# Products with v in quarters of the array for two pairs at once, in two accumulators, in an fp32 attention and feed-forward kernel

## The chip, the cores and the metric

One core of one Trainium2 chip runs the whole kernel. The metric is the device time of one execution in microseconds, the median of several runs. A profile of one further execution stands beside it.

## The reference

```python
def _attn_ref(q, k, v):                       # 8 x 12 heads, 448 keys, 64 wide
    scores = scale * np.matmul(q, k.transpose(0, 1, 3, 2)) - np.log(S)
    attn = 1.0 / (1.0 + np.exp(-scores))
    return np.matmul(attn, v).astype(np.float32)

def _moe_ref(x, w_in, w_out):                 # 3584 x 768, 768 x 2048, 2048 x 768
    h = x @ w_in
    g = np.maximum(0.01 * h, h)
    return (g @ w_out).astype(np.float32)

# attention's output, heads side by side, is x of the second
```

The attention has sigmoids in place of a softmax, so that no sum over the keys has to be divided by.

## The kernel before

The kernel has three stages. Attention is the first: 48 pairs of heads, two pairs in a round, 24 rounds. The two other stages are the two products of the feed-forward part, computed by schemes with fewer block products than the plain one; their weights need sums of blocks, and these are made by VectorE (DVE) during attention (the generator `prep`, tiles `wr`, `wd`, `ws`, `w`). So do the sums of attention's results (`x`, `x_s`), which the second stage multiplies.

In a pair, one head lies on partitions 0 to 63 and the other on 64 to 127 (`heads`). Q and k (`qk`, raw) are split by ScalarE (ACT, a cast, `high`) and DVE (a subtraction, `low`) into a high and a low part (`qks`). The 448 keys are three tiles of 128 and a last one of 64. The work of a pair on TensorE (PE) has three kinds:

- `scores`: for a key tile, high x high, high x low and low x high for both heads, six matmuls of 64 rows and 128 columns of the array (64*128 in a profile), into a PSUM tile `sc` of two banks. ACT makes the sigmoid into `s`.
- `attn_v`: v with `s` in plain fp32, three key tiles for two heads. A matmul has 128 rows and 64 columns (128*64): the two heads use the two halves of the array's columns. Both pairs of a round accumulate in one PSUM tile `pv`, a bank each.
- `last_scores` and `last_v`: the last 64 keys of both pairs together, in quarters of the array (64*64), from the raw q and k, in plain fp32. `last_scores` of a round is for the pairs of the next round.

An fp32 matmul shows as two records in a profile, each two passes of 448 columns; the texts below call such a record of all parts of the array together a pass.

A round has five slots: scores of pair x, scores of pair y, `attn_v` of x, of y, and then `last_scores` for the next round and `last_v`. The first round has another order, x's products standing ahead of y's scores. Beside the slots `later` puts casts, loads and copies into a slot ahead of its work: z and w, the pairs of the next round, are cast in slots 2 and 3 and their low parts made in slots 3 and 4, and ACT copies `pv` to an `x` tile in slot 0 of the next round (`Block.keep`). In each slot `prepare` gives DVE further work, as much as the table `ROOM` says (us by slot): sums of `x` first, then steps of `prep`. A finished weight unit brings four casts for ACT in slot 3 and four subtractions for DVE in slot 4 (`w`, "weight lows" below).

All engines and queues run their instructions in this written order. PSUM has four buffers of two banks in attention, used in turn; the second stage uses the same eight banks for its accumulators (`f`). Loads and stores stand in SyncE's queue (SP).

Of the kernel before, what the change touches and what calls it, by code (L numbers as in the profile page):

```python
# [11 lines left out]
F32 = mybir.dt.float32  # L12
# [6 lines left out]
P = 128  # L19


ROOM = 1.7, 2.2, 2.1, 0.7, 0.2
SLOT, READ, STEP, LATE = 2.4, 1.09, 0.7, 1.1
CAST, SOON, HOLD = 3, 2, 4
PAUSE = 1
IDLE = 7


TILES, MORE, LAST, JOIN = 13, 3, 6, 6
RESULTS = 8  # L30
ROTS = 3
EARLY, FIRST, SOON2, JOINT = 12, 9, (2, 5), 26
# [89 lines left out]
def attn_ffn_kernel(ctx: ExitStack, tc: tile.TileContext, qk, v, w_in, w_out, out):  # L122
# [13 lines left out]
    S = qk.shape[3]  # L136
    NP = qk.shape[0] // B
    D = P // 2
    NK = 4
# [9 lines left out]
    heads = [slice(j * D, j * D + D) for j in range(2)]  # L149
# [22 lines left out]
    mm, dma = pinned(nc.tensor.matmul), pinned(nc.sync.dma_start)  # L172
# [8 lines left out]
    def add(to, x, y):  # L181
        vec(out=to, in0=x, in1=y, op=ALU.add)
# [14 lines left out]
    def later(slots, *fns, first=False):  # L197
        at(now + slots, 0 if first else 5, *fns)

    def slot(work=None, behind=()):  # L200
        nonlocal now
        todo = sorted(chores.pop(now, ()), key=lambda x: x[0])
        for rank, fn in todo:
            if rank not in behind:
                fn()
        if work is not None:
            work()
        for rank, fn in todo:
            if rank in behind:
                fn()  # L210
        now += 1
# [72 lines left out]
    ps = ExitStack()  # L284
# [37 lines left out]
    def drop(t, slots=1):  # L322
# [3 lines left out]
    attn = ExitStack()  # L326
    vs = attn.enter_context(tc.tile_pool(name="vs", bufs=4, reuse_waits="tile"))
    shift(attn, "pad1", 64)
    raws, spl, ats, made1, wr3 = (attn.enter_context(tc.tile_pool(name=name, bufs=bufs, reuse_waits="tile")) for name, bufs in (
        ("raws", 4), ("spl", 2), ("at", 6), ("sums", 1), ("wr3", 1)))  # L330
    warm = shift(ctx, "warm", 32, "right")
    tiles(ctx, "r", "right", TILES)
    shift(ctx, "pad2", 64, "right")
# [161 lines left out]
    xs, sums = {}, []  # L495

    HALVES = slice(0, S // 2), slice(S // 2, S)
# [7 lines left out]
    class Pair:  # L505


        def __init__(self, i):
            self.i, self.part = i, part(i)
            self.a = []  # L510

        def load_qk(self):
            self.raw = raws.tile([P, 2, S], F32, tag="qk", name=f"qk_{self.i}")
# [10 lines left out]

        def load_v(self):
            n = 2 * NK - 2 * (self.part == 1)
            t = vs.tile([P, 2 * NK * D + 2 * S], F32, tag="v", name=f"v_{self.i}")
            self.v = t[:, :2 * NK * D].rearrange("p (a b) -> p a b", a=2 * NK)
            self.room = t[:, 2 * NK * D:2 * NK * D + 2 * S].rearrange("p (a b) -> p a b", a=2)
            dma(out=self.v[:, :n], in_=v[self.i, :, :n])  # L530

        def high(self, how=None):
# [16 lines left out]
                    for x in HALVES:  # L549
                        sub(low[:, 0, x], self.raw[:, 0, x], high[:, 0, x])  # L550

        def scores(self, h):
            todo, acts = [], []
            for c in range(2 * h, min(2 * h + 2, NK - 1)):
                ps = psum("s", f"sc_{self.i}_{c}")

                for cols in HALVES if self.i == h == 0 else (slice(0, S),):
                    for m, (kp, qp) in enumerate(((0, 0), (0, 1), (1, 0))):
                        for j, me in enumerate(heads):
                            todo.append((c, (m > 0 and c + 1, m, cols.start), dict(  # L560
                                out=ps[:, j, cols], lhsT=self.parts[me, kp, 1, c * P:c * P + P],
                                rhs=self.parts[me, qp, 0, cols], start=m == 0 and cols.start == 0,
                                stop=m == 2 and cols.stop == S, skip_group_check=True)))
                acts.append((c, ps))
            if self.i == h == 0:
                todo.sort(key=lambda x: x[1])
            for n, (c, ps) in enumerate(acts):
                for x in todo if self.i == h == 0 and n == 0 else [x for x in todo if x[0] == c and (self.i or h)]:
                    mm(**x[2])
                self.a.append(self.attn(c, ps))  # L570

        def attn(self, c, ps, s=None):
# [5 lines left out]
        def last_scores(self):  # L578

            ps = psum("s", f"sc_{self.i}_{NK - 1}")  # L580
            for j, me in enumerate(heads):
                for y, rows in zip(pairs[self.i:], heads):
                    mm(ps[rows, j, :S], lhsT=y.raw[me, 1, S - D:], rhs=y.raw[me, 0], start=True, stop=True, skip_group_check=True)
            self.last = self.attn(NK - 1, ps, pairs[self.i + 1].room)

        def attn_v(self):
            mate = pairs[self.i - 1]
            if self.part == 1:
                self.both = psum("s", f"pv_{self.i}")
            self.pv = (self if self.part == 1 else mate).both[:, self.part - 1]  # L590
            for c in range(NK - 1):
                for j, me in enumerate(heads):
                    mm(self.pv[me, :S], lhsT=self.v[:, (NK - 1) * j + c, :], rhs=self.a[c][:, j], start=c == 0, stop=False,
                       skip_group_check=True)

        def last_v(self):

            x = pairs[self.i - 1]
            for j, me in enumerate(heads):
                for y, rows in ((x, heads[0]), (self, heads[1])):  # L600
                    mm(y.pv[me, :S], lhsT=self.v[rows, 2 * NK - 2 + j, :], rhs=x.last[rows, j],
                       start=False, stop=True, skip_group_check=True)
            block = Block(self.i // 2)
            later(1, lambda: block.keep(x.both), first=True)
            at(now + 2, 8, block.start)

    class Block:
# [7 lines left out]
        def keep(self, pv):  # L615
            xs[self.name] = grab(f"x_{self.p}_{self.name}", F32)
            copy(out=xs[self.name], in_=pv[:, :, :S])

        def store(self, n, t, *gone):

# [72 lines left out]
    pairs[3].load_qk()  # L693
    psum = banks("ps_a", dict(s=(4, 2)))

    def whole(x):
        x.scores(0)
        x.scores(1)

    def ending(x, y):  # L700

        if y is not None:
            y.last_scores()
        x.last_v()

    unread = psum("s", "unread")[:, 0]
    for _ in range(IDLE):
        mm(unread[heads[0], :S // 4], lhsT=zeros[:, :D], rhs=zeros, start=True, stop=True)
    slot(lambda: pairs[0].scores(0))
    slot(lambda: pairs[0].scores(1))  # L710
# [19 lines left out]

    for r in range(rounds):
        x, y, *more = pairs[2 * r:2 * r + 6]
        works = [lambda: whole(x), lambda: whole(y), x.attn_v, y.attn_v, lambda: ending(y, more[0] if more else None)]
        if r == 0:

            works = [works[2], works[1], lambda: None, *works[3:]]
        if more:
            z, w = more[:2]
            later(0, z.load_v)
            later(1, w.load_v)  # L740
            later(2, z.high)
# [440 lines left out]
```

## Time and profile before

| | |
|---|---|
| median of 3 runs (lowest to highest) | 1013.57 us (1013.32 to 1014.59) |
| profiled execution | 1013.27 us |
| its span, first to last instruction | 1011.5 us |
| PE, DVE, ACT busy | 1006.9, 853.2, 586.2 us |
| attention, until the second stage's first matmul | 249.31 us |

The span is what the profile's rows are measured in, from its start; the 1.8 us between span and time lie around it. Busy time of PE counts matmuls, which are pipelined, so that a stall shorter than a matmul's own duration does not show as idle time; starts show it. Matmuls and their weight loads (PEld) stand apart.

### The profile page before, as it was taken

The page shows a single profiled execution, that of the slowest core. Times are in us where ns is not written, and L with a number is a line of the kernel's source. Part 1 is how long each engine was busy: PE and PEld are TensorE (multiplying, and loading weights), DVE is VectorE, ACT ScalarE, POOL GpSimd, SP SyncE. Part 2 cuts the span into 40 slices and gives each one's busy share as a digit, 9 for nine tenths or more (in the row PEclk, how much of TensorE's full clock was granted, in tenths as well). Part 3 has the DMA queues.
Part 4 walks back from the last instruction along what each step waited for, and adds up shares of the span by engine and source line. Part 5 has one row for each costly group of instructions (what it writes and reads, how often), then busy time and mean ns, then how long its engine had stood idle before and what let it go on. Part 6 is the DMA issues. An engine that isn't in the chain of part 4 may idle for free.

```text
span 1011.5 us, 15201 instructions
## 1 busy us (share of the span) xinstructions
PE 1006.9 (100%) x5642; PEld 844.5 (83%) x5642; DVE 853.2 (84%) x1116; ACT 586.2 (58%) x710; POOL 0.3 (0%) x5
## 2 busy tenths in 40 slices
PE   9999999999999999999999999999999999999998
PEld 5555455555999999999999999999999999999998
DVE  5888888887898779888867778799998999999886
ACT  7888888887644454445453655575453456635431
POOL 0000000000000000000000000000000000000000
PEclk9999999999999999999999999999999999999999
DMA  9799899998988997799789979967738698775643
GB/s 326 269 337 370 298 379 324 361 336 276 382 302 241 348 321 266 246 384 311 246 268 315 322 238 362 409 222 255 269 118 321 250 361 326 241 279 164 215 171 109
DMA packets 142025, 291.79 MB, mean 288 GB/s; under 512 B 11136, under 2 KB 71680, under 8 KB 141952
## 3 DMA queue, kind: packets, MB, share of 16 engines
q1 hardware_dynamic: 141088, 290.02, 81.9%
q8 instruction: 44, 0.72, 0.3%
q10 hardware_dynamic: 864, 0.80, 0.2%
q14 instruction: 29, 0.24, 0.1%
HBM read 189.33 MB, written 101.45 MB: 287 GB/s over the span
## 4 chain that ended last, share of the span: by engine, by line
PE 99%; DMA 0%; DVE 0%; ACT 0%; DVEq 0%; issue 0%
PE f L159 38%; PE a L159 36%; PE pv L159 13%; PE sc L159 11%; PE e_z L159 0%; DMA qk<-in_qk 0%; PE e_a L159 0%; DVE o L159 0%; ACT qks L159 0%; DVEq L1178 0%
## 5 line engine op out<-in xcount | busy, mean ns | idle before, releaser
L159 PE MATMUL a<-gh,w 128*128 128x448 f32 x1224 | 342.9, 361 | 0.0
L159 PE MATMUL f<-xh,w 128*128 128x448 f32 x960 | 270.9, 361 | 0.0
L159 PEld LDWEIGHTS a<-gh,w 128*128 128x128 f32 x1224 | 229.3, 187 | 16.9
L159 PE MATMUL a<-gl,w 128*128 128x448 f32 x540 | 196.0, 363 | 0.0
L159 PEld LDWEIGHTS f<-xh,w 128*128 128x128 f32 x960 | 179.9, 187 | 14.3 <-issue 0.7
L159 PE MATMUL f<-xl,w 128*128 128x448 f32 x480 | 174.2, 363 | 0.0
L159 ACT CAST gh<-g 128x896 fp32r<-128x896 f32 x80 | 75.4, 942 | 123.3 <-DVE g L159 108.7
L159 DVE TENSOR_TENSOR h<-h,f 128x896 f32<-128x896 f32 x88 | 95.5, 1085 | 50.4 <-PE f L159 50.2
L159 ACT ACTIVATE s<-sc 128x896 f32<-128x896 f32 x144 | 119.8, 956 | 3.1 <-PE sc L159 3.1
L159 PE MATMUL pv<-s,v 128*64 128x448 f32 x576 | 113.8, 543 | 0.0
L159 ACT COPY h<-f 128x896 f32<-128x896 f32 x56 | 50.1, 910 | 96.5 <-PE f L159 75.2
L159 PEld LDWEIGHTS a<-gl,w 128*128 128x128 f32 x540 | 101.3, 188 | 5.4
L159 DVE TENSOR_TENSOR w<-w 128x768 fp32r<-128x768 f32 x112 | 104.5, 953 | 1.0 <-ACT w L159 1.0
L159 PEld LDWEIGHTS sc<-qks 64*128 64x128 f32 x876 | 79.9, 186 | 23.2 <-issue 16.9
L159 ACT CAST w<-w 128x768 fp32r<-128x768 f32 x112 | 93.1, 832 | 4.0 <-DMA w<-t 4.0
L159 PE MATMUL sc<-qks 64*128 64x448 f32 (+1 forms) x876 | 94.8, 367 | 0.2 <-ACT qks L159 0.2
L159 PEld LDWEIGHTS f<-xl,w 128*128 128x128 f32 x480 | 90.1, 188 | 4.6
L159 PEld LDWEIGHTS pv<-s,v 128*64 128x64 f32 x576 | 39.1, 137 | 63.2 <-issue 54.3
L159 PE MATMUL f<-xh,ws 128*128 128x448 f32 x320 | 91.5, 361 | 0.0
L159 DVE TENSOR_TENSOR gl<-g,gh 128x896 fp32r<-128x896 f32 x72 | 78.3, 1088 | 5.0 <-ACT gh L159 4.5
L159 ACT CAST xh<-xl 128x896 fp32r<-128x896 f32 x64 | 60.3, 944 | 35.5 <-DMA xl<-xd 22.2
L159 DVE TENSOR_TENSOR qks<-qk,qks 128x832 fp32r<-128x832 f32 (+3 forms) x51 | 49.2, 972 | 37.1 <-ACT qks L159 33.9
(79 smaller groups left out, 1072.8 us busy)
## 6 DMA issues: line engine op xcount, KB each, us to landing
w<-t SPq DMA_DIRECT2D x112, 384.0 KB, 4.7
g<-g SPq DMA_DIRECT2D x81, 448.0 KB, 5.8
xl<-xd SPq DMA_DIRECT2D x64, 448.0 KB, 6.4
g<-h SPq DMA_DIRECT2D x64, 448.0 KB, 6.0
qk<-in_qk SPq DMA_DIRECT2D x46, 448.0 KB, 5.6
xd<-x_s SPq DMA_DIRECT2D x36, 448.0 KB, 6.8
xd<-x SPq DMA_DIRECT2D x28, 448.0 KB, 6.6
wr<-in_w_in SPq DMA_DIRECT2D x24, 512.0 KB, 6.6
```

What stands on the lines that cost most here:

```text
L159: return lambda *args, **kw: tc.keep_in_program_order(issue(*args, **kw))
```

## The change

Pairs x and y of a round are multiplied with v together. Each key tile's product is divided into two half products over 64 keys each: `attn_v(c, n)` issues, for both heads, x with one half of the rows and y with the other, four matmuls on four quarters of the array (64*64). With n = 0 the halves go into the accumulator `both[0]`, with n = 1, where x and y have changed halves, into `both[1]`, so that each bank gets its matmuls from one half of the rows only. `last_v` adds to `both[1]`. ACT copies `both[0]` to the `x` tile in slot 4 (`Block.keep`), and DVE adds `both[1]` to it in slot 0 of the next round (`Block.add`).

The score tiles of x and y alternate. `last_scores` stands ahead of the products now, in the first round also, and the first round's x products are no longer ahead of y's scores. A round takes nine PSUM tiles in turn, before it was eight. Last-key sigmoids have tiles of their own (`ends`), and the v tiles are smaller. `ROOM` is 1.2, 2.2, 1.9, 0.7, 0.6, and of the tiles for `x` one more lies on the right and one less on the left.

```diff
-ROOM = 1.7, 2.2, 2.1, 0.7, 0.2
+ROOM = 1.2, 2.2, 1.9, 0.7, 0.6
...
-TILES, MORE, LAST, JOIN = 13, 3, 6, 6
+TILES, MORE, LAST, JOIN = 14, 2, 6, 6
...
-            self.last = self.attn(NK - 1, ps, pairs[self.i + 1].room)
-
-        def attn_v(self):
-            mate = pairs[self.i - 1]
-            if self.part == 1:
-                self.both = psum("s", f"pv_{self.i}")
-            self.pv = (self if self.part == 1 else mate).both[:, self.part - 1]
-            for c in range(NK - 1):
-                for j, me in enumerate(heads):
-                    mm(self.pv[me, :S], lhsT=self.v[:, (NK - 1) * j + c, :], rhs=self.a[c][:, j], start=c == 0, stop=False,
-                       skip_group_check=True)
+            s = ends.tile([P, 2, S], F32, tag="e", name=f"s_{self.i}_{NK - 1}")
+            self.last = self.attn(NK - 1, ps, s)
+
+        def attn_v(self, c, n):
+
+            x = pairs[self.i - 1]
+            if c == 0:
+                self.both.append(psum("s", f"pv_{x.i}_{n}"))
+            for j, me in enumerate(heads):
+                for m, (y, rows) in enumerate(((x, heads[1 - n]), (self, heads[n]))):
+                    mm(self.both[n][me, m, :S], lhsT=y.v[rows, (NK - 1) * j + c, :], rhs=y.a[c][rows, j],
+                       start=c == 0, stop=n == 0 and c == NK - 2, skip_group_check=True)
+            if c == NK - 2 and n == 0:
+                self.block = Block(self.i // 2)
+                later(1, lambda: self.block.keep(self.both[0]), first=True)
...
             for j, me in enumerate(heads):
-                for y, rows in ((x, heads[0]), (self, heads[1])):
-                    mm(y.pv[me, :S], lhsT=self.v[rows, 2 * NK - 2 + j, :], rhs=x.last[rows, j],
+                for m, (y, rows) in enumerate(((x, heads[0]), (self, heads[1]))):
+                    mm(self.both[1][me, m, :S], lhsT=self.v[rows, 2 * NK - 2 + j, :], rhs=x.last[rows, j],
                        start=False, stop=True, skip_group_check=True)
-            block = Block(self.i // 2)
-            later(1, lambda: block.keep(x.both), first=True)
+            block = self.block
+            later(1, lambda: block.add(self.both[1]), first=True)
             at(now + 2, 8, block.start)
...
+
+        def add(self, pv):
+            add(xs[self.name], xs[self.name], pv[:, :, :S])
...
         x, y, *more = pairs[2 * r:2 * r + 6]
-        works = [lambda: whole(x), lambda: whole(y), x.attn_v, y.attn_v, lambda: ending(y, more[0] if more else None)]
+        def scores(*todo):
+            for z, c in todo:
+                z.scores(c)
+
+        def products(*todo):
+            if more and todo[0] == (0, 0):
+                more[0].last_scores()
+            for c, n in todo:
+                y.attn_v(c, n)
+            if todo[-1][0] == NK - 2 and todo[-1][1]:
+                y.last_v()
+
+        works = [
+            lambda: scores((x, 0), (y, 0), (x, 1)), lambda: scores((y, 1), (x, 2), (y, 2)),
+            lambda: products((0, 0), (1, 0)), lambda: products((0, 1), (1, 1), (2, 0)), lambda: products((2, 1))]
         if r == 0:
-
-            works = [works[2], works[1], lambda: None, *works[3:]]
+            works[:2] = lambda: scores((y, 0)), lambda: scores((y, 1), (y, 2))
```

The order on PE in the first round, before. The names are tiles with their numbers: `sc_3` are last-key scores, `sc_0` to `sc_2` the score tiles of pair 1, `pv` the products, `qk_244` and `qk_257` the raw q and k of pairs 2 and 3:

```order
L159 MATMUL pv_317<-s_0_296,v_232 64x448 x2
L159 MATMUL pv_317<-s_1_298,v_232 64x448 x2
L159 MATMUL pv_317<-s_2_307,v_232 64x448 x2
L159 MATMUL sc_0_328<-qks_254 128x448 x6
L159 MATMUL sc_1_329<-qks_254 128x448 x6
L159 MATMUL sc_2_346<-qks_254 128x448 x6
L159 MATMUL pv_317<-s_0_336,v_246 64x448 x2
L159 MATMUL pv_317<-s_1_344,v_246 64x448 x2
L159 MATMUL pv_317<-s_2_353,v_246 64x448 x2
L159 MATMUL sc_3_369<-qk_244 64x448
L159 MATMUL sc_3_369<-qk_257 64x448
```

The same place of the changed kernel, where `qk_247` and `qk_260` are pairs 2 and 3:

```order
L159 MATMUL sc_0_321<-qks_257 128x448 x6
L159 MATMUL sc_1_334<-qks_257 128x448 x6
L159 MATMUL sc_2_343<-qks_257 128x448 x6
L159 MATMUL sc_3_354<-qk_247 64x448
L159 MATMUL sc_3_354<-qk_260 64x448
L159 MATMUL sc_3_354<-qk_247 64x448
L159 MATMUL sc_3_354<-qk_260 64x448
L159 MATMUL pv_0_361<-s_0_299,v_235 64x448
L159 MATMUL pv_0_361<-s_0_328,v_249 64x448
```

The last-key scores of pairs 2 and 3 have moved from behind all twelve products of the first round to a place ahead of them.

The order on DVE at the end of a round with weight lows, before (`qks` are the low parts of z and w, `w_0` the weight lows, `wd` and `wr` steps of the weight preparation, `x_s` sums of results):

```order
L159 TENSOR_TENSOR qks_936<-qk_833,qks_936 128x832
L159 TENSOR_TENSOR w_0_0_209<-ws_1_798,w_0_0_209 128x256
L159 TENSOR_TENSOR w_0_0_209<-wd_1_591,w_0_0_209 128x128
L159 TENSOR_TENSOR w_0_1_213<-ws_1_798,w_0_1_213 128x384
L159 TENSOR_TENSOR w_0_2_217<-ws_1_798,w_0_2_217 128x384
L159 SCALAR_TENSOR_TENSOR wd_2_878<-wr_2_0_713,wd_2_878 128x512
```

The same place of the changed kernel, where `x_10_1161<-x_10_1161,pv_1_1148` is the addition of the second accumulator:

```order
L159 TENSOR_TENSOR qks_1142<-qk_1033,qks_1142 128x832
L159 TENSOR_TENSOR w_0_0_212<-ws_1_880,w_0_0_212 128x256
L159 TENSOR_TENSOR w_0_0_212<-wd_1_685,w_0_0_212 128x128
L159 TENSOR_TENSOR w_0_1_216<-ws_1_880,w_0_1_216 128x384
L159 TENSOR_TENSOR w_0_2_220<-ws_1_880,w_0_2_220 128x384
L159 TENSOR_TENSOR x_11_771<-x_s_719,x_11_771 128x896
L159 TENSOR_TENSOR x_10_1161<-x_10_1161,pv_1_1148 128x896
```

An addition that reads PSUM now stands behind the weight lows and one further instruction; before, none of DVE's instructions in attention read PSUM.

The order on DVE at the end of attention, of the changed kernel (`xl_0` is the first low part of the second stage):

```order
L159 SCALAR_TENSOR_TENSOR x_s_3353<-x_s_3335,x_11_3125 128x896
L159 TENSOR_TENSOR xl_0_3263<-xl_0_3263,xh_0_3339 128x896
L159 TENSOR_TENSOR w_3_0_215<-ws_7_3172,w_3_0_215 128x256
L159 TENSOR_TENSOR w_3_0_215<-wd_7_2947,w_3_0_215 128x128
L159 TENSOR_TENSOR w_3_1_219<-ws_7_3172,w_3_1_219 128x384
L159 TENSOR_TENSOR w_3_2_223<-ws_7_3172,w_3_2_223 128x384
L159 SCALAR_TENSOR_TENSOR wd_0_3234<-wr_0_1_3132,wd_0_3234 128x512
L159 TENSOR_TENSOR x_21_3373<-x_21_3373,pv_1_3360 128x896
```

Here the last unit's weight lows, which before were made a round earlier, and the last addition have come between the low part and the second stage.

## Rows read from the trace of the kernel before

**Rows 1.** The page: busy time of the engines; the chain that ended last, by engine
```profile
PE 1006.9 (100%) x5642; PEld 844.5 (83%) x5642; DVE 853.2 (84%) x1116; ACT 586.2 (58%) x710; POOL 0.3 (0%) x5
...
PE 99%; DMA 0%; DVE 0%; ACT 0%; DVEq 0%; issue 0%
```
**Rows 2.** Windows: length, then PE, PEld, DVE, ACT, POOL busy, granted clock, DMA share, GB/s
```profile
16.22:239.89 223.67, 223.67 (x1676) 119.88 (x1673) 187.79 (x326) 189.48 (x253) 0.00 (x0) 1.00 0.93 330
249.31:1010.00 760.69, 758.86 (x3796) 710.76 (x3792) 651.28 (x767) 378.76 (x435) 0.00 (x0) 1.00 0.79 276
```
**Rows 3.** PE in order of time, one round: start, duration, instruction, count
```profile
101.40 4.73 PE L159 MATMUL pv<-s,v 128*64 128x448 f32 x24
106.06 0.98 PE L159 MATMUL sc<-qk 64*64 64x448 f32 x8
106.86 0.93 PE L159 MATMUL pv<-v 64*64 64x448 f32 x8
107.72 3.91 PE L159 MATMUL sc<-qks 64*128 64x448 f32 x36
111.57 0.97 PE L159 MATMUL pv<-s,v 128*64 128x448 f32 x4
```
**Rows 4.** PE's weight loads in that round, and one in the next products
```profile
104.08 0.14 PEld L159 LDWEIGHTS pv<-s,v 128*64 128x64 f32 x2 [0.23 <-issue]
...
105.21 0.14 PEld L159 LDWEIGHTS pv<-s,v 128*64 128x64 f32 x2 [0.23 <-issue]
...
106.49 0.15 PEld L159 LDWEIGHTS pv<-v 64*64 64x64 f32 x4 [0.22 <-issue]
106.86 0.15 PEld L159 LDWEIGHTS pv<-v 64*64 64x64 f32 x4 [0.22 <-issue]
...
111.99 0.14 PEld L159 LDWEIGHTS pv<-s,v 128*64 128x64 f32 x2 [0.23 <-issue]
```
**Rows 5.** DMA issues from 5.9 to 6.3: size, us from issue to landing
```profile
qk<-in_qk SPq DMA_DIRECT2D x1, 448.0 KB, 7.7
```
**Rows 6.** PE, DVE and SP in order of time, the program's start
```profile
1.03 2.88 PE L159 MATMUL unread<-zeros 128*64 128x112 f32 x14 [1.03 <-DVE zeros L682]
...
5.98 0.33 SPq L159 DMA_DIRECT2D qk<-in_qk  x1
...
6.79 0.98 PE L159 MATMUL sc<-qk 64*64 64x448 f32 x8
6.89 1.02 DVE L159 TENSOR_TENSOR qks<-qk,qks 128x832 fp32r<-128x832 f32 x1
...
14.56 0.98 PE L159 MATMUL sc<-qk 64*64 64x448 f32 x8
```
**Rows 7.** Groups of DVE's instructions: count, busy, mean ns
```profile
L159 DVE TENSOR_TENSOR h<-h,f 128x896 f32<-128x896 f32 x88 | 95.5, 1085 | 50.4 <-PE f L159 50.2
...
L159 DVE SCALAR_TENSOR_TENSOR wd<-wr,wd 128x512 int32<-128x512 int32 x48 | 33.2, 691 | 1.2
...
L159 DVE TENSOR_SCALAR wd<-wr 128x512 int32<-128x512 int32 x23 | 9.7, 422 | 0.0
```
**Rows 8.** ACT and DVE in order of time, the round from 117.89
```profile
118.88 4.98 ACT L159 ACTIVATE s<-sc 128x896 f32<-128x896 f32 x6
...
123.67 1.73 ACT L159 CAST qks<-qk 128x832 fp32r<-128x832 f32 x2
...
124.66 1.96 DVE L159 TENSOR_TENSOR qks<-qk,qks 128x832 fp32r<-128x832 f32 x2 [1.53 <-ACT qks L159]
...
126.54 0.42 DVE L159 TENSOR_TENSOR w<-ws,w 128x256 fp32r<-128x256 f32 x1
...
128.01 0.69 DVE L159 SCALAR_TENSOR_TENSOR wd<-wr,wd 128x512 int32<-128x512 int32 x1
```
**Rows 9.** DVE and PE in order of time, the end of attention
```profile
246.71 1.09 DVE L159 TENSOR_TENSOR xl<-xl,xh 128x896 fp32r<-128x896 f32 x1 [0.72 <-ACT xh L159]
...
249.31 0.48 PE L159 MATMUL f<-xh,w 128*128 128x448 f32 x1
```

More of the change, by code (lines that the diff above doesn't have):

```diff
@@ L328, in attn_ffn_kernel @@
     shift(attn, "pad1", 64)
-    raws, spl, ats, made1, wr3 = (attn.enter_context(tc.tile_pool(name=name, bufs=bufs, reuse_waits="tile")) for name, bufs in (
-        ("raws", 4), ("spl", 2), ("at", 6), ("sums", 1), ("wr3", 1)))
+    raws, spl, ats, ends, made1, wr3 = (attn.enter_context(tc.tile_pool(name=name, bufs=bufs, reuse_waits="tile")) for name, bufs in (
+        ("raws", 4), ("spl", 2), ("at", 6), ("ends", 2), ("sums", 1), ("wr3", 1)))
     warm = shift(ctx, "warm", 32, "right")
@@ L509, in __init__ @@
             self.i, self.part = i, part(i)
-            self.a = []
+            self.a, self.both = [], []
         def load_qk(self):
@@ L526, in load_v @@
             n = 2 * NK - 2 * (self.part == 1)
-            t = vs.tile([P, 2 * NK * D + 2 * S], F32, tag="v", name=f"v_{self.i}")
-            self.v = t[:, :2 * NK * D].rearrange("p (a b) -> p a b", a=2 * NK)
-            self.room = t[:, 2 * NK * D:2 * NK * D + 2 * S].rearrange("p (a b) -> p a b", a=2)
+            self.v = vs.tile([P, 2 * NK, D], F32, tag="v", name=f"v_{self.i}")
             dma(out=self.v[:, :n], in_=v[self.i, :, :n])
@@ L550, in split, with scores @@
                         sub(low[:, 0, x], self.raw[:, 0, x], high[:, 0, x])
-        def scores(self, h):
+        def scores(self, *blocks, halves=False):
             todo, acts = [], []
-            for c in range(2 * h, min(2 * h + 2, NK - 1)):
+            for c in blocks:
                 ps = psum("s", f"sc_{self.i}_{c}")
-                for cols in HALVES if self.i == h == 0 else (slice(0, S),):
+                acts.append((c, ps))
+                for cols in HALVES if halves else (slice(0, S),):
                     for m, (kp, qp) in enumerate(((0, 0), (0, 1), (1, 0))):
                         for j, me in enumerate(heads):
-                            todo.append((c, (m > 0 and c + 1, m, cols.start), dict(
+                            todo.append(((m > 0 and c + 1, m, cols.start), dict(
                                 out=ps[:, j, cols], lhsT=self.parts[me, kp, 1, c * P:c * P + P],
@@ L563, in scores @@
                                 stop=m == 2 and cols.stop == S, skip_group_check=True)))
[L564 to L569, printed above, removed]
+            for _, x in sorted(todo, key=lambda x: x[0]) if halves else todo:
+                mm(**x)
+            for c, ps in acts:
                 self.a.append(self.attn(c, ps))
@@ L694, in attn_ffn_kernel @@
     psum = banks("ps_a", dict(s=(4, 2)))
[L696 to L704, printed above, removed]
     unread = psum("s", "unread")[:, 0]
@@ L708, in attn_ffn_kernel @@
         mm(unread[heads[0], :S // 4], lhsT=zeros[:, :D], rhs=zeros, start=True, stop=True)
-    slot(lambda: pairs[0].scores(0))
-    slot(lambda: pairs[0].scores(1))
+    slot(lambda: pairs[0].scores(0, 1, halves=True))
+    slot(lambda: pairs[0].scores(2))
     slot(pairs[0].last_scores)
```

## Prediction

> **What bounds the kernel now.** I read the page first: PE is busy all the span, DVE 84%, ACT 58%, and the chain that ended last is 99% PE [rows 1]. A busy PE need not be a PE without waits, so the rounds come next. Attention is 24 rounds; 22 of them, from 16.22 to 239.89, take 223.67 us, 10.17 each, and DVE is busy for 187.79 / 22 = 8.5 us of one [rows 2]. Behind attention PE is busy for 758.86 of 760.69 us and has no slack in which to make good a delay. So each ns that PE saves or waits in attention is a ns of the kernel.
>
> A round is then cut by kinds, from start to start [rows 3]: scores 107.72 to 111.57 (3.85 us), products with v 101.40 to 106.06 (4.66), last-key scores to 106.86 (0.80), last-key products to 107.72 (0.86). That is 10.17 and leaves no wait. A pass of the products is (105.21 - 104.08) / 3 = 0.376 us, whereas the first lasts 0.42 (111.57 to 111.99), and from the last pass's start to the next kind's are (106.06 - 105.21) - 0.376 = 0.47 [rows 3, 4]. Thus a change of shape in this place costs 0.05 + 0.10 = 0.15 us. A pass of quarters (64*64) is 0.37 too: loads of four at 106.49 and 106.86.
>
> **What the change removes.** Before: 12 matmuls a round, two at once on halves of the array, in two passes, that is 12 passes; after: 24 matmuls on quarters, four at once, again 12 passes. Quarters are not filled better than halves, and a pass has the same price in both shapes. One change of shape a round goes, since last-key scores, products and last-key products now all are 64*64: 3.85 + 0.80 + 12 x 0.376 + 0.86 = 10.02 against 10.17, **0.15 us a round, 3.5 us in 23 rounds**. That is all there is to gain on PE.
>
> Here a rule speaks against the change. The Trainium skill, "TensorE: Matmul & The Clock Gate", Part 3, "What overlaps and what doesn't", says that a weight load overlaps running matmuls only where the row groups differ. By it the loads of a quarter pass would stand open, as the next pass uses the same rows: four loads last 0.15 us [rows 4], 12 x 24 x 0.15 = 43 us. The trace contradicts it: at 106.49 and 106.86 four loads start while passes run, and the passes still follow at 0.37. I go by the rows.
>
> **What it adds: a wait at the start.** Last-key scores now stand ahead of the products, in the first round too. There they read the raw q and k of pairs 2 and 3. Pair 3's load is issued at 5.98 and lands 7.7 us later, at 13.7 [rows 5, 6]; the order of the loads ahead of it is unchanged. Before, PE came to these scores at 14.56, having done x's and y's products meanwhile [rows 6]. After: the first last-key scores at 6.79, 0.05 + 0.86 later, at 7.70, y's scores (their low part is ready at 7.91, needed about 0.5 us into them), which are half of a round's 18 pairs of score matmuls and take 2.0 us; so PE is at pair 3 by about 9.8 and stands still until 13.7. The products that would fill the time stand behind the wait. From 13.7: 0.80 + 12 x 0.376 + 0.86 = 6.17, so the second round begins at 19.87 and not at 16.22: **+3.65 us**. In later rounds I put it at nothing: those loads are issued a round ahead.
>
> **A second accumulator to read.** ACT copies the first one, as it copied the only one before; DVE adds the second. The nearest row is a 128x896 addition with one operand in PSUM, h<-h,f, 1.09 us [rows 7]; 24 of them are 26 us of DVE, hidden if nothing waits for them. But nine PSUM tiles a round now go through four buffers, so the second accumulator's buffer is that of the fourth score tile of the next round. Call a round's start T, the next one's T'. The fourth of six tiles begins halfway through 3.85 us of scores, at T + 1.93; the addition must be done by then. The last product ends at about T + 0.1, so where DVE is free the addition runs to T + 1.2, and nothing is lost.
>
> DVE is late in the seven rounds (in the order) where it also makes the low parts of a weight unit. ACT's order is now z's cast, last-key sigmoid, w's cast, weight casts, so that w's cast and these casts come one sigmoid, 0.81 us (4.98 / 6, overlapped), later. Put into the round from 117.89 [rows 8]: w's cast ends at 126.2 instead of 125.4; DVE's w low starts then and frees DVE after 0.94, at 127.14; the four weight lows take 1.47 (126.54 to 128.01), so DVE is free at 128.61, 0.7 us into the next round. An addition at once would end at T' + 1.85 with its signal, 0.08 before the deadline. But other work stands between. With 0.08 of overlap off each duration: a 512-wide step of 0.34 three times, of 0.61 twice, two small steps (0.79) once, a sum of 1.00 once [rows 7]. Together 4.0, less 7 x 0.08: **+3.5 us**. Bounds: 2, if the weight casts are earlier than I put them, and 6, if sums delay DVE in its light rounds too.
>
> **The end of attention.** The first matmul of the second stage takes the bank of the last second accumulator and so waits for its addition. Last round, T = 239.89: without last-key scores PE ends at T + 3.85 + 0.05 + 12 x 0.376 + 0.86 = T + 9.27. DVE's xl low starts at T + 6.82, once ACT's cast is done (246.71) [rows 9]; then 1.00 for it, 1.47 for four weight lows, 0.61 for one step, 1.09 of addition and 0.05 of signal: T + 11.05. **+1.8 us** (1.2 at the least, the addition alone). Before, the stage began without a wait: 249.31 is T + 9.42, the sum above with its change of shape.
>
> **At no cost:** keeping the first accumulator on ACT, which ends before the third score tile needs its bank at T' + 1.3 even behind the weight casts (about T' + 0.5); the `ends` pool and the other places of tiles; the weight preparation that `ROOM` moves out of attention, since DVE behind it is busy for 651 of 761 us [rows 2]. If that cover is gone, it is a stall of some tenths in single slots.
>
> **Sum.** 3.65 - 3.5 + 3.5 + 1.8 = +5.4 us. On the profiled execution's 1013.27 that is **1018.7**; the median of the runs shown is 1013.57, 0.3 more, and a difference below 0.2% (2 us) can't be told from none.
>
> **Rivals.** (1) PE's clock falls in the wait at the start, some 3 us without a matmul. The program's first 14 steps of 112 columns take 2.88 us, about 0.19 each, where a quarter of a 448-column pass of 0.376 is 0.094: the lower level; from 6.79 on last-key scores have the usual pitch [rows 6]. Such a stretch again, at least 2.5 us and at most 5.8 (1.03 to 6.79), costs half its length, 1.2 to 2.9; I take 2: 1020.7. Against: there PE had done nothing at all before, here it has worked for 9 us. The Trainium skill, same page, "What's actually happening", says that the default is the throttled state and activity releases it; no run here shows a fall in the middle of a program. (2) Pair 3 lands before 9.8: 1015.1. Only the order of issue speaks for my number, and it is unchanged. (3) The additions are never late, because DVE's steps are shorter than their rows: 1015.2. (4) DVE is late in its light rounds as well: its load rises by 1.0 to 9.5 of 10.02 us, and 0.3 us in 16 more rounds is 1023.5. (5) Loads stand open, or quarters run one after another: over 1050; rows 4 speak against it. (6) The other side: a pass of quarters is cheaper than one of halves. It decides from 5.4 / (23 x 12) = 0.020 us a pass on: below 0.356 the kernel isn't slower, at 0.34 it is 1009. Against: the 0.37 of last-key passes.
>
> **How the numbers follow.** My forecast 0.64 (own range 1017 to 1020.5), rival 1 0.10, 2 0.07, 3 0.06, 4 0.05, 5 0.02, 6 0.06. From 1015.0 to 1021.5 only 4, 5 and 6 are left out. Rivals 2 and 3 end within 0.2%: faster 0.06, same 0.14, slower 0.80.
>
> **What would show it.** In the profile after: rounds of 10.02 us wherever DVE is free; PE idle between about 10.5 and 13.7, with a load of q and k as releaser; score tiles waiting for DVE's addition from PSUM in seven rounds, by 0.3 to 0.9; the first f behind such an addition, near 254.7 instead of 249.31; the same pitch after it. I am wrong if pair 3's last-key scores start near 9.8, if quarter passes are not 0.376, or if the fourth score tile never waits.

## The result, and the profile after

| | before | after |
|---|---|---|
| median (lowest to highest) | 1013.63 us (1013.32 to 1015.6), 6 runs | **1021.76 us** (1020.37 to 1024.52), 6 runs |
| ratio to before, 95% interval | | **1.0078**, 1.0062 to 1.0094 |
| profiled execution, its span | 1013.27, 1011.5 us | 1024.52, 1022.7 us |

The kernel is slower by 8 us, where 5 were forecast; the time lies 0.26 us above the range's upper end of 1021.5. Most of the profile is as before. The page after, busy time of the engines and the chain that ended last, as in [rows 1]:

```profile
PE 1009.3 (99%) x6218; PEld 851.2 (83%) x6218; DVE 877.2 (86%) x1140; ACT 587.6 (57%) x710; POOL 0.3 (0%) x5
...
PE 89%; DMA 4%; ACT 3%; DVE 3%; issue 1%; SPq 0%; DVEq 0%; ACTq 0%
```

A chain that was 99% PE now runs through loads, ACT and DVE as well. The waits of PE in the whole execution after (for whom, us in total, times, the longest) say which:

```profile
PE sc L159 <- DMA qk<-in_qk: 2.9, 1, 2.9
PE sc L159 <- DVE x L159: 2.6, 6, 0.8
PE f L159 <- DVE x L159: 1.7, 1, 1.7
PE f L159 <- DVE xl L159: 1.3, 1, 1.3
```

The first three are the waits that the prediction named: pair 3's load, the additions, the first `f`. The fourth was not foreseen. These are idle times; a matmul's own duration covers part of each stall, so the starts have to be read. PE after in order of time, the program's start, as in [rows 6]:

```profile
7.23 0.98 PE L159 MATMUL sc<-qk 64*64 64x448 f32 x8
8.14 2.23 PE L159 MATMUL sc<-qks 64*128 64x448 f32 x18
10.29 0.96 PE L159 MATMUL sc<-qk 64*64 64x448 f32 x2
14.20 1.02 PE L159 MATMUL sc<-qk 64*64 64x448 f32 x3 [2.94 <-DMA qk<-in_qk]
...
15.12 8.08 PE L159 MATMUL pv<-s,v 64*64 64x448 f32 x55
23.13 1.08 PE L159 MATMUL sc<-qks 64*128 64x448 f32 x8
```

Pair 2's last-key scores start, and pair 3's wait until 14.20, as forecast (13.7). But the second round begins at 23.13 and not at 19.87. From 14.20 on, the 6.17 us of work that the prediction added up took 8.93. Windows of 2 us of the same stretch (columns as in [rows 2]; the granted clock is the third from the end) show why:

```profile
10.00:12.00 2.00, 1.26 (x6) 0.19 (x2) 0.00 (x0) 2.00 (x4) 0.00 (x0) 1.00 1.01 414
12.00:14.00 2.00, 0.00 (x0) 0.00 (x0) 1.02 (x1) 0.74 (x1) 0.00 (x0) 0.75 1.03 400
14.00:16.00 2.00, 1.80 (x12) 0.91 (x16) 0.00 (x0) 0.00 (x0) 0.00 (x0) 0.50 1.03 404
16.00:18.00 2.00, 2.00 (x16) 0.82 (x12) 0.26 (x1) 1.69 (x2) 0.00 (x0) 0.50 0.22 80
18.00:20.00 2.00, 2.00 (x16) 0.93 (x11) 0.76 (x1) 0.00 (x0) 0.00 (x0) 0.54 0.00 0
20.00:22.00 2.00, 2.00 (x28) 1.07 (x24) 0.00 (x0) 0.22 (x1) 0.00 (x0) 1.00 0.00 0
```

PE stood still, its granted clock fell to 0.50 (1.2 GHz), stayed there for some 5.5 us behind the wait and then returned to 2.4 GHz. 8.93 - 6.17 = 2.76 us were lost. That is rival 1.

Then the rounds. PE after, one plain round and a long one:

```profile
73.71 3.90 PE L159 MATMUL sc<-qks 64*128 64x448 f32 x36
77.54 0.98 PE L159 MATMUL sc<-qk 64*64 64x448 f32 x8
78.34 5.44 PE L159 MATMUL pv<-s,v 64*64 64x448 f32 x56
83.72 2.08 PE L159 MATMUL sc<-qks 64*128 64x448 f32 x18
86.58 0.68 PE L159 MATMUL sc<-qks 64*128 64x448 f32 x4 [0.78 <-DVE x L159]
...
88.60 0.98 PE L159 MATMUL sc<-qk 64*64 64x448 f32 x8
...
94.78 1.48 PE L159 MATMUL sc<-qks 64*128 64x448 f32 x12
```

The plain round takes 83.72 - 73.71 = 10.01 us (10.17 before), the long one 94.78 - 83.72 = 11.06. DVE after, at the border of these two rounds, as in [rows 8]:

```profile
82.03 1.03 DVE L159 TENSOR_TENSOR qks<-qk,qks 128x832 fp32r<-128x832 f32 x1 [0.55 <-ACT qks L159]
82.97 0.42 DVE L159 TENSOR_TENSOR w<-ws,w 128x256 fp32r<-128x256 f32 x1
83.30 0.28 DVE L159 TENSOR_TENSOR w<-wd,w 128x128 fp32r<-128x128 f32 x1
83.51 1.02 DVE L159 TENSOR_TENSOR w<-ws,w 128x384 fp32r<-128x384 f32 x2
84.44 1.08 DVE L159 TENSOR_TENSOR x<-x_s,x 128x896 f32<-128x896 f32 x1
85.44 1.08 DVE L159 TENSOR_TENSOR x<-x,pv 128x896 f32<-128x896 f32 x1
```

W's low part, four weight lows, a sum, and only then the addition (`x<-x,pv`), which ends at 86.5; the fourth score tile starts at 86.58. The 22 rounds from 23.13 on last 224.84 us, against 223.67 [rows 2]: 22 x 10.007 = 220.15, and 4.7 more in seven long rounds.

PE and DVE after at the end of attention, as in [rows 9]:

```profile
257.85 1.08 DVE L159 TENSOR_TENSOR x<-x,pv 128x896 f32<-128x896 f32 x1
...
258.98 0.47 PE L159 MATMUL f<-xh,w 128*128 128x448 f32 x1 [1.68 <-DVE x L159]
```

The first `f` is at 258.98 (249.31 before) and 11.01 us behind the last round's start, 1.74 us more than the 9.27 that the prediction gives a last round without a wait (9.26 in experiment 6).

### The profile page after: what moved, and what is told of

The parts are those of the page before. It is cut to its first block, busy times and chain, and to the rows that moved or that the text cites. A ratio compares the mean times of both kernels' runs of the same rounds, so it can differ in the third digit from the quotient of the medians.

```text
span 1022.7 us, 16379 instructions
## 1 busy us (share of the span) xinstructions
PE 1009.3 (99%) x6218; PEld 851.2 (83%) x6218; DVE 877.2 (86%) x1140; ACT 587.6 (57%) x710; POOL 0.3 (0%) x5
## 4 chain that ended last, share of the span: by engine, by line
PE 89%; DMA 4%; ACT 3%; DVE 3%; issue 1%; SPq 0%; DVEq 0%; ACTq 0%
PE a L159 36%; PE f L159 35%; PE pv L159 9%; PE sc L159 8%; ACT s L159 2%; DMA xl<-xd 2%; DMA qk<-in_qk 1%; DVE x L159 1%; ACT qks L159 1%; DVE w L159 1%; DMA t<-ws 1%; PE e_z L159 0%; DVE qks L159 0%; DMA v<-in_v 0%; DVE wd L159 0%
## 5 line engine op out<-in xcount | busy, mean ns | idle before, releaser
L159 ACT ACTIVATE s<-sc 128x896 f32<-128x896 f32 x168 | 142.7, 940 | 32.0 <-PE sc L159 31.8
L159 PE MATMUL pv<-s,v 64*64 64x448 f32 x1344 | 134.1, 543 | 0.0
L159 PEld LDWEIGHTS pv<-s,v 64*64 64x64 f32 x1344 | 53.0, 135 | 75.9 <-issue 67.6
L159 PE MATMUL sc<-qks 64*128 64x448 f32 (+1 forms) x876 | 97.1, 370 | 3.0 <-DVE x L159 2.6
L159 ACT ACTIVATE h<-h 128x896 f32<-128x896 f32 x56 | 53.1, 952 | 49.6 <-DVE h L159 49.3
```

The costliest lines, as they stand in the source:

```text
L159: return lambda *args, **kw: tc.keep_in_program_order(issue(*args, **kw))
```

## The experiments

All are edits of the changed kernel. The table has what each profile gives, in us: the start of the second round, the 22 rounds that follow, the first `f` behind the start of the last round, and the span that is left from there. Ratios to before, with their intervals, stand in the text.

| kernel | second round | 22 rounds | to first f | rest | median |
|---|---|---|---|---|---|
| before | 16.22 | 223.67 | 9.42 | 762.2 | 1013.6 |
| after | 23.13 | 224.84 | 11.01 | 763.8 | 1021.76 |
| 1 old place in the first round | 16.73 | 224.91 | 11.01 | 762.8 | 1016.70 |
| 2 filled wait | 21.17 | 225.00 | 11.01 | 763.4 | 1021.61 |
| 2 half filled | 20.11 | 224.92 | 11.00 | 762.6 | 1020.42 |
| 3 after, again | 21.57 | 224.89 | 11.01 | 762.2 | 1022.02 |
| 4 weight lows later | 22.17 | 221.99 | 11.01 | 762.2 | 1019.20 |
| 5 steps moved (and 1) | 16.34 | 221.11 | 10.63 | 762.0 | 1012.65 |
| 6 other accumulators | 22.17 | 224.87 | 9.26 | 763.6 | 1021.69 |
| 6 with 1, 4 and 5 | 16.67 | 221.78 | 9.27 | 764.6 | 1013.62 |
| 1, 4 and 5 alone | 16.54 | 221.58 | 10.99 | 762.8 | 1013.38 |
| 6 mirrored, with 1, 4 and 5 | 16.75 | 221.99 | 9.26 | 764.0 | 1013.29 |
| 7 even rounds | 16.62 | 220.15 | 9.26 | 764.5 | 1011.65 |
| 7 and the last order | 16.90 | 220.15 | 9.26 | 762.8 | **1010.02** |

**1. The place of the first last-key scores.**

```diff
-            if more and todo[0] == (0, 0):
+            if more and todo[0] == (0, 0) and r > 0:
                 more[0].last_scores()
...
+                if r == 0:
+                    more[0].last_scores()
                 y.last_v()
```

> In the first round alone the last-key scores of pairs 2 and 3 go back behind the products, just ahead of the last-key products; all other rounds stay as in the changed kernel. Theory (the wait for pair 3's load and the half clock behind it both belong to the new place of these scores): no wait at 10 to 14 us, granted clock 1.0 throughout from 7 us on, second round at 16.1 to 16.5 us and not at 23.1, and 6.4 us off the median: 1015.4. Rival (the clock falls for another reason, such as the many quarter passes or the program's age, and the profiled execution alone was hit): the clock falls here also, only the wait of 3.65 us goes, 1018.1. The seven long rounds and the 1.7 us at the end of attention stay in both.

1016.70, ratio 1.0028 (1.0018 to 1.0039): 5.1 us off. PE of this kernel in order of time:

```profile
10.56 4.74 PE L159 MATMUL pv<-s,v 64*64 64x448 f32 x48
15.12 0.93 PE L159 MATMUL sc<-qk 64*64 64x448 f32 x8
15.87 0.93 PE L159 MATMUL pv<-s,v 64*64 64x448 f32 x8
16.73 3.90 PE L159 MATMUL sc<-qks 64*128 64x448 f32 x36
```

Twelve quarter passes run from 10.56 on with no wait and at full clock in every window of this stretch, so that neither the quarters nor their place in the program lowers it. The second round is at 16.73 and not 23.13, 6.40 us earlier, as much as the theory had it. The median alone would not decide: 1016.70 lies between the theory's 1015.4 and the rival's 1018.1. The granted clock does, for the theory. The medians moved by less (5.1), since the changed kernel's profiled execution is the longest of its six: its mean granted clock over the whole span is 0.997, the others have 0.998 or 0.999.

**2. The filled wait, and a half.** The number is 17 in one kernel and 9 in the other.

```diff
             ps = psum("s", f"sc_{self.i}_{NK - 1}")
+            for _ in range(17 * (self.i == 2)):
+                for j, me in enumerate(heads):
+                    mm(ps[:, j, :S], lhsT=pairs[1].parts[me, 0, 1, :P], rhs=pairs[1].parts[me, 0, 0], start=True, stop=True,
+                       skip_group_check=True)
```

> Ahead of the first round's last-key scores, 17 pairs of matmuls that are of no use (64*128, written into the last-key scores' own PSUM tile and overwritten by them) keep PE at work for about 3.6 us, while pair 3's load is on its way. Theory (standing still lowered PE's clock): the load still sets the start at about 14, but the granted clock stays at 1.0 behind it and the second round begins at about 20.4 and not at 23.1: 2.7 us off, 1019.1. Rival (the clock falls by what comes after the wait, the last-key scores and the quarter passes, or by the program's age): it falls here too, the second round stays at 23, 1021.8.

> As the run with filling matmuls, 9 pairs of them in place of 17, so that PE stands still for 1.7 to 2.2 us ahead of the last-key scores of pair 3 and not for 3 to 3.5. Theory (the clock falls when PE stands still for long): granted clock 1.0 throughout, second round 6.2 us behind pair 3's landing, 20.4 to 21.2. Rival (any wait in this place lowers it): clock 0.5 behind the wait, second round later by 1 to 2.8. And for the first fill, whose median did not fall: if its later loads (pair 3 at 14.96) come from the filling, they land after 14.6 here too; if from one execution, at 14.1 to 14.3, and the median is 1019 to 1020.

With 17 pairs the granted clock is 1.00 in every window behind the wait, and pair 3's scores start at 14.95, the second round 6.22 us behind them. With 9 pairs, PE of that kernel in order of time:

```profile
11.95 0.96 PE L159 MATMUL sc<-qk 64*64 64x448 f32 x2
13.95 0.60 PE L159 MATMUL sc<-qk 64*64 64x448 f32 x3 [1.03 <-DMA qk<-in_qk]
...
20.11 1.08 PE L159 MATMUL sc<-qks 64*128 64x448 f32 x8
```

and its windows:

```profile
12.00:14.00 2.00, 0.96 (x7) 0.19 (x5) 1.03 (x1) 0.57 (x1) 0.00 (x0) 1.00 1.04 397
14.00:16.00 2.00, 2.00 (x23) 1.30 (x27) 0.00 (x0) 1.02 (x2) 0.00 (x0) 1.00 1.02 398
```

1.03 us of idle time (less than the 1.7 to 2.2 expected) left the clock at 1.00, and 20.11 - 13.95 = 6.16 us is the forecast's 6.17 to a hundredth. So the work behind the wait was forecast rightly, the loss behind it is the clock's, and it comes from PE standing still: the same scores and products stand behind the wait in all these kernels. In ten executions with a filling the mean clock is 0.999 or 1.0, in all 21 executions of the changed kernel (both runs), of the weight lows moved (4) and of the first other order of accumulators (6), which have the wait unfilled, it is 0.996 to 0.999. The traces of the last two show the fall too: 22.17 - 14.31 - 6.17 = 1.69 us were lost in experiment 4, 22.17 - 14.35 - 6.17 = 1.65 in experiment 6.

The medians follow only in part. Half filled: 1020.42, ratio 1.0066 (1.0053 to 1.0078), 1.6 below the changed kernel run beside it; the two intervals overlap, so that it is the profile that shows the gain. Filled: 1021.61, ratio 1.0075 (1.0062 to 1.0088), no gain, a miss. In its profile the second round is 2.0 us earlier than in the changed kernel's (21.17 against 23.13), and not 2.8, since pair 3's scores started 0.75 later (14.95 against 14.20). Two things ended together there: pair 3's load landed at 14.96, 0.8 later than in the changed kernel, and the 17 pairs, which had begun late behind a late load of pair 1, kept PE busy until 14.95. 0.8 us more went in a wait for a low part (`xl`) at 450. As the half filled kernel had pair 3's data by 13.95, a filling as such does not delay loads. Whether the other executions had the same delays stays open.

**3. The changed kernel again, unedited.**

> The changed kernel again, unedited, beside the others for a second profile and a median on the same chip. Theory: 1021.5 within 1.0; wait for pair 3 to about 14.2, granted clock 0.5 for 1 to 5 us behind it; seven long rounds of the same lengths to 0.02 us; 1.7 us at the first f; the second stage without a wait of over 1 us in it, 762.3 to 762.8 (the 1.44 us at 451 belong to one execution). Rival (the wait at 451 belongs to the change): 763.5 or more, with a wait for DVE at 190 us behind the first f.

1022.02, ratio 1.0077 (1.0064 to 1.009). The seven long rounds agree with the first profile's to 0.02 us and the first `f` exactly; the rest of the span is 762.2 as before. The wait of 1.3 us for `xl` is not there: at this place DVE waits for a reload of `h` (`h_m`, by DMA) for 3.52 us in the first profile, for 1.96 here and for 1.26 in the kernel before, and up to 1.96 it costs nothing. It is no part of the change. Windows of this execution:

```profile
12.00:14.00 2.00, 0.13 (x4) 0.13 (x7) 1.02 (x1) 0.63 (x1) 0.00 (x0) 0.90 1.03 404
14.00:16.00 2.00, 2.00 (x12) 0.87 (x16) 0.00 (x0) 0.31 (x1) 0.00 (x0) 0.50 1.00 391
16.00:18.00 2.00, 2.00 (x20) 1.00 (x16) 0.59 (x1) 1.38 (x2) 0.00 (x0) 0.75 0.16 57
```

The clock fell here too, but for a shorter time; pair 3's scores start at 13.87, so that the second round at 21.57 means 7.70 - 6.17 = 1.53 us lost, in place of 2.76.

**4. The weight lows behind the addition.**

```diff
-        at(cast + 1, 9, lambda: parts(False), lambda: prepared.add((0, u)))
+        at(cast + 2 if cast + 2 < base else cast + 1, 9, lambda: parts(False), lambda: prepared.add((0, u)))
```

> The four weight lows of DVE go one slot later, from the last slot of a round to the first of the next, behind the addition of the second accumulator; the last unit keeps its place. Theory (the seven long rounds are long since the weight lows and what stands behind them hold up the addition, whose PSUM buffer the fourth score tile needs): these seven rounds take 10.01 us like the others, 4.7 us off: 1017.1. Rival (DVE's load as a whole makes the additions late, wherever the lows stand): the waits move to the next round's casts and low parts, other rounds become long by 0.3 to 0.6, and no more than 2 us is gained: 1019.8 or more.

1019.20, ratio 1.0051 (1.0038 to 1.0063). The 22 rounds lose 2.85 of their 4.7 us: between theory and rival. Of the 1.84 us left, 1.2 are three rounds that still wait for an addition, as the rival had it. DVE of this kernel, at its longest round's start (PE's round starts at 122.55, its fourth score tile at 124.92):

```profile
122.05 1.02 DVE L159 TENSOR_TENSOR qks<-qk,qks 128x832 fp32r<-128x832 f32 x1
122.98 0.42 DVE L159 TENSOR_TENSOR ws<-wd,ws 128x256 f32<-128x256 f32 x1
123.44 0.42 DVE L159 TENSOR_TENSOR ws<-ws,wd 128x256 f32<-128x256 f32 x1
123.78 1.08 DVE L159 TENSOR_TENSOR x<-x,pv 128x896 f32<-128x896 f32 x1
```

The lows are gone, but now two steps of the weight preparation from the last slot's room (0.6) stand ahead of the addition, behind a low part of w that is itself late. Another 0.46 us of this kernel is a wait that nobody foresaw: in the round from 153.14 the last-key scores stand still until a load of q and k lands, at 157.40. The prediction had put such waits at nothing behind the first round. The changed kernel's two profiles have none there.

**5. DVE's further work moved from the last slot to the first instead**, on top of experiment 1, with the lows left where they were.

```diff
-ROOM = 1.2, 2.2, 1.9, 0.7, 0.6
+ROOM = 1.8, 2.2, 1.9, 0.7, 0.0
```

> As the first run (last-key scores of the first round behind the products), and DVE's further work taken out of the last slot, the weight lows staying ahead of the addition. Theory (of the 0.39 to 1.05 us of a long round, 0.34 to 1.00 are the step between lows and addition, and only about 0.2 a round comes from elsewhere): the seven rounds take 10.05 to 10.25, together 0.8 to 1.6 above seven light ones and not 4.7; 1013.3 against the first run's 1016.7. Rival (the steps move into places that make the addition as late, DVE being full): 1015 or more.

1012.65, ratio 0.9993 (0.9983 to 1.0003): 4.05 below experiment 1. The 22 rounds are 0.96 above 22 plain ones and not 4.76. So of the long rounds' 4.7 us, 3.8 went with that work (steps, and in one round a sum); the lows alone nearly fit ahead of the addition, as the prediction's chain said. (0.4 us at the end of attention went too, 10.63 in place of 11.01.)

**6. The accumulators of the second stage.** The first `f` takes a buffer that was read early:

```diff
     psum = banks("ps_f", {f"acc{n}": (1, 2) for n in range(4)})
+    for n in (1, 2, 3, 0):
+        psum(f"acc{n}", f"place{n}")
```

> The accumulators of the second stage take the four PSUM buffers in another order, so that the first matmul gets banks that were read early and only the last of the first four needs the banks of the last second accumulator. Theory (1.7 us at the end of attention are a wait for the last addition on DVE, through its banks): the first f starts 1.7 us earlier behind the last pv, 1.7 off: 1020.1. Rival (the first f waits for x low parts or weights on DVE and ACT anyway, which stand beside the addition): it starts at most 0.5 us earlier, or a wait of the same size comes within the first microseconds of the second stage, 1021.3 or more.

1021.69, ratio 1.008 (1.0068 to 1.0093): no gain, as the rival had it. The profile shows both halves of it. The first `f` comes 9.26 us behind the round's start, 1.75 earlier than before the edit, and 385 us later a wait has come. Waits of PE from 600 to 660 us, this kernel:

```profile
PE a L159 <- ACT h L159: 1.1, 1, 1.1
```

The third stage's accumulators lie in the same buffers, and its first one now had to wait for a later read of the second stage. The next three kernels have experiments 1, 4 and 5 in one, the first with this order, the second without it, the third with a mirrored order, which was meant to keep the third stage's predecessors.

> Three edits of the first runs together, and DVE's further work moved out of the last slot of a round (the table's last number 0.0 in place of 0.6, its first 1.8 in place of 1.2), so that nothing but z's and w's low parts stands ahead of the addition: last-key scores behind the products in the first round, weight lows behind the addition, accumulators of the second stage in another order. Theory (the changed kernel is slow by four places alone, and a round of 10.007 is its gain): every round 10.01 us, second round at 16.1 to 16.7, first f 9.25 us behind the last round's start, at about 246, second stage 762.3 as before: about 1010, below before by 3 to 4 us. Rival (DVE's load of 9.5 in 10.0 us has no room wherever its work stands): other rounds become long, 1012 or more.

> The kernel of the run beside it without the other order of accumulators. Theory (1.7 us of wait at the end of attention are a loss of their own, and the gain of the other order was lost in its first run to a wait near 640 us that belongs to one execution): first f 1.1 to 1.7 us later than there, and the median 1.1 to 1.7 above it, about 1011.3. Rival (the other order of accumulators brings a wait into the second or third stage): the first f comes later than there by as much, but the medians agree within 0.4.

> Last-key scores of the first round behind the products, weight lows behind the addition, no further work of DVE in the last slot (first number of the table 1.8, last 0.0), and the second stage's four accumulators in mirrored order on the PSUM buffers, with the third stage's four groups mirrored as well, so that each of its accumulators follows the same accumulator of the second stage as in the changed kernel. Theory (the other order of accumulators saved 1.7 us at the first f, and lost it at the start of the third stage, since there an accumulator came upon another predecessor): first f 9.3 us behind the last round's start, no wait above 0.5 us near the third stage's first matmul, 1.3 to 1.7 below the 1013.4 of the same kernel without it: 1011.9. Rival (the third stage's start waits for ACT or a load whichever accumulator comes first, and only its time of day moved): the wait of 1.2 to 1.5 us is there again, 1013.4.

1013.62, 1013.38 and 1013.29, ratios 0.9996 (0.9987 to 1.0005), 0.9996 (0.9987 to 1.0004) and 0.9997 (0.9988 to 1.0005): none differs measurably from before, and all lie 1.4 to 3.6 us above their theories. The second's rival came true, its median agrees with the first's to 0.24: the order gains 1.7 at the first `f` and loses most of it again near 633; so does the mirrored one, whose rival came true in its number. ACT and PE of it at that place show whom the third stage's first `a` meets:

```profile
633.01 0.91 ACT L159 ACTIVATE h<-f 128x896 f32<-128x896 f32 x1
...
633.98 0.47 PE L159 MATMUL a<-gh,w 128*128 128x448 f32 x1 [1.09 <-ACT h L159]
```

That read is the last one of the second stage's last accumulator: the mirrored order did not keep the old predecessor. And three rounds in each of the three kernels stayed long, by 0.3 to 0.6, since their second score tile waits for a low part that DVE made late. That weight lows and 1.8 us of further work met in one round there is the reading that experiment 7 tests. The first and the third kernel have a fourth long round, by 0.33 and 0.46, of another kind: as in experiment 4, its last-key scores wait for a load of q and k, which lands at 152.11 and 152.39.

**7. Even rounds.** On top of the mirrored kernel, weight lows are charged to DVE's room:

```diff
-ROOM = 1.8, 2.2, 1.9, 0.7, 0.0
+ROOM = 1.8, 2.4, 2.1, 0.8, 0.0
...
         def parts(high):
+            nonlocal credit
+            credit -= 1.47 * (not high)
```

> The kernel of the run beside it, with the weight lows charged to DVE's room (1.47 us less further work after them) and the table 1.8, 2.4, 2.1, 0.8, 0.0, so that rounds with weight lows get less and the others more. Theory (the last long rounds, four by 0.3 to 0.55, come where further work and weight lows meet in one round): all rounds within 0.1 of 10.007, another 1.0 to 1.4 off: 1010.7. Rival (the other rounds are as full, 7.1 of further work with 2.9 of low parts and addition in 10.0 us): they become long, 1012 or more.

1011.65, ratio 0.9978 (0.9969 to 0.9987), faster than before, and 1.64 below the mirrored kernel run beside it. All 22 rounds are at 10.007. The theory's 1010.7 started from a gain of the mirrored order that did not come; the wait of 1.1 us at the third stage is still there. The last kernel changes only the order of the accumulators, to `(3, 2, 0, 1)` with the third stage as it was:

> The kernel with even rounds, except that the second stage's accumulators take the PSUM buffers in an order in which only those of the first two change places, and the third stage's groups are not mirrored: the first matmul of the second stage comes upon a buffer that was read early, the second accumulator, a slot later, upon the one that DVE adds from, and the third stage's first accumulator upon the same as in the changed kernel. Theory (the wait of 1.2 us at the third stage's first matmul came from the buffers' order): first f 9.3 us behind the last round's start, at about 246, no wait near 631, 1.2 below the 1011.65 of the kernel with even rounds: 1010.4, 3.2 below before. Rival (what the first f no longer waits for, the second accumulator does, or the third stage waits as before): 1011.4 to 1012.

**1010.02, ratio 0.9962** (0.9948 to 0.9975): 3.7 us below the kernel before, as the theory had it (1010.4). The order of the buffers, then, and not the third stage as such, made that wait. Its waits of PE, the whole execution:

```profile
PE unread L159 <- DVE zeros L686: 1.0, 1, 1.0
PE f L159 <- DVE xl L159: 0.5, 1, 0.5
PE sc L159 <- DVE qks L159: 0.3, 1, 0.3
```

and its windows over 22 rounds and over the second and third stage:

```profile
16.90:237.04 220.14, 220.14 (x2204) 124.36 (x2200) 206.31 (x340) 190.71 (x253) 0.00 (x0) 1.00 0.94 329
246.30:1009.07 762.77, 758.95 (x3796) 711.18 (x3792) 655.97 (x777) 378.08 (x435) 0.00 (x0) 1.00 0.79 277
```

No wait for a load of q and k, none for an addition, none at the third stage's start. The changed kernel's four losses are undone and its gain of 3.5 us stands, with quarters, two accumulators and last-key scores in front from the second round on.

## Why the prediction was wrong

The step that failed is the clock. The text put it at a chance of 0.10, as rival 1, with the reason that at the program's start "PE had done nothing at all before, here it has worked for 9 us". That reason does not hold: 2.94 us without a matmul brought the granted clock down to 0.50, in this profile and, shorter, in the second. Its price was well read: 2 us was taken, 1.2 to 2.9 as bounds, and 2.76, 1.53, 1.69 and 1.65 were measured in the four profiles with the unfilled wait. With it in the forecast the number would have been 1020.7. A second term was mis-sized: the late additions cost 4.7 us, where 3.5 were summed up. With only one of the two misses the time would have stayed inside the stated range (1021.76 less 1.2, or less 1.5). The Trainium skill, "TensorE: Matmul & The Clock Gate", has a section, "HAM oscillation — how this bites in real kernels", that tells of the same thing, a kernel in which PE waits for a load between bursts and begins each burst throttled; the prediction cited the section on the default state alone. The traces agree with it here: 0.50 was granted behind idle times of 2.53 to 2.95 us in all four profiles.

Step by step, with the second profile (21.57, 224.89, 11.01, 762.2) against the forecast's 19.87, 223.9 (22 x 10.02 + 3.5), 11.05 and 762.2:

- **One change of shape less, -3.5.** Right. Plain rounds take 10.007 us where 10.02 were summed up. Quarter passes cost what half passes did, and their weight loads stay hidden: 22 rounds in 220.14 us leave no room for 0.15 us a pass. Rivals 5 and 6 fall.
- **The wait at the start, +3.65.** Right. Pair 3 landed at 14.15 and 13.82 (forecast 13.7), and the half filled kernel shows the 6.17 us of work behind it. Rival 2 falls.
- **The late additions, +3.5.** The mechanism is right (seven rounds, those with weight lows, and the step in between as the cause); the size is 4.7, within the bounds of 2 to 6. In the round shown the fourth score tile was late by 86.58 - 83.72 - 1.92 = 0.94 us, 1.92 being half of the 3.83 from 73.71 to 77.54; 0.92 were forecast. But the round is longer by 1.05. From the fourth score tile to the last-key scores the long round takes 88.60 - 86.58 = 2.02 us, where a plain one takes 1.91: the score matmuls lose about 0.1 us when they start again, as they do at a change of shape [rows 3, 4]. All seven rounds show it (0.10 to 0.12), 0.75 us together, a term that the sum lacked. The fourth tile's lateness adds up to 3.93 us. Five rounds have it as forecast to 0.03; two have 0.17 more, since DVE has two steps to do ahead of w's low part. Rival 3 falls; so does rival 4, since all other rounds are plain.
- **One of those two rounds.** DVE after, ahead of the round from 53.16:

```profile
50.83 0.42 DVE L159 TENSOR_SCALAR wd<-wr 128x512 int32<-128x512 int32 x1
51.28 0.43 DVE L159 TENSOR_SCALAR wd<-wd 128x512 f32<-128x512 f32 x1
51.63 1.02 DVE L159 TENSOR_TENSOR qks<-qk,qks 128x832 fp32r<-128x832 f32 x1
```

  W's low part begins 1.53 us ahead of the round, behind two steps; the forecast had 126.2 for a round that would start at 127.91, 1.71 ahead.
- **The end of attention, +1.8.** Right: 11.01 - 9.27 = 1.74.
- **Nothing elsewhere.** Right for this kernel: 762.2 us are left behind the first `f` in the second profile, as before. The 1.44 us at 451 in the first belong to one late reload.

The sum of the misses: 1.5 of clock, 0.2 of landing and wait, 1.2 of additions, less 0.3 of plain rounds, is 2.6 of the 3.06 between 1018.7 and 1021.76; another 0.36 is that the median of before lies above the profiled execution that the sum was made against. The single edits give the same account of the medians. Without wait and clock loss 3.0 us remain above before, and -3.5 + 4.7 + 1.7 = 2.9; without all four losses the kernel is 3.7 faster.

## What to carry to other kernels

Price a wait of a busy PE twice: for its length and for the clock that it may cost behind it, and ask whether other matmuls can stand in the gap; half of it filled was enough here to hold the clock. Where an engine must give a buffer back by a due time, look at every instruction that stands ahead of the reading one in its order, and move those that nobody waits for: here small steps of weight preparation cost more than the addition itself. An edit of buffers has to be followed to the next stage that uses the same buffers, or a stall is only moved.

## What the runs showed of the hardware

- After idle times of 2.53 and 2.94 us (second and first profile of the changed kernel) the granted clock stood at 0.50 for some 3 and 5.5 us of work; after 1.03 us it stayed at 1.00. The loss does not follow the length of the gap: 2.94 us cost 2.76 in one profile, 2.95 us cost 1.65 in another (experiment 6).
- Score matmuls that had stood still for DVE's addition lost 0.10 to 0.12 us on starting again, in each of seven rounds (1.05 us of round for 0.94 of lateness in the one shown), though their shape was the same.
